# A cross-attention and gated-MLP kernel: the splits of the scores and of the state attention share three buffers, a group's two splits stand together, and the state block's input is split in halves

## The chip, the cores and the metric

The kernel runs on one core of a Trainium2 chip. A core has TensorE (PE in the profile, with PEld for its weight loads), VectorE (DVE), ScalarE (ACT), GpSimd (POOL) and SyncE (SP), which here issues nearly all transfers. The metric is the device time of one execution in microseconds; lower is better.

## The reference

For each of 8 batches and 8 heads there are 512 rows of `x` and 32 rows of `state`, 64 wide. The attention goes both ways: `xread = softmax(scale * x @ state^T) @ state`, and `sread = softmax(scale * state @ x^T) @ x`. Both are joined along the rows, the heads are laid side by side (512 wide, 544 rows per batch, 4352 in all), and two dense stages follow in float32:

```
...
    gate = 1.0 / (1.0 + np.exp(-(x @ w_gate)))
    val = x @ w_val
    return (gate * val @ w_out).astype(np.float32)
...
    h = x @ w_in
    r = np.maximum(h, 0.0)
    g = r * r
    return (g @ w_out).astype(np.float32)
```

The first has 1536 hidden columns, the second 2048.

## The kernel before

Every float32 matmul is made of three: both operands are split into a high part (fp32r, an ACT cast) and the rest (a subtraction), and `mm3` (lines 182 to 184) runs high by high, high by low and low by high.

**The first dense stage** is a list of 108 units. A unit is one slice of 128 hidden columns of one block of rows. Units 0 to 95 are blocks of `x` (512 rows, one batch each; batches 0 to 3 in two halves of six units, then batches 4 to 7 with twelve units each); units 96 to 107 are the state block, the 256 state rows of all batches. `front_x` makes gate and value in PSUM (`psg`, `psv`), a sigmoid on ACT (line 550), a product and its split on DVE and ACT (lines 556, 189, 190); `back1` multiplies by the output weights into four accumulators (`acc`). The units of `x` never form `xread`: the state rows are multiplied by the weights beforehand (`state_weights`, stored by `store_g`, loaded again by `load_g`, split by `split_gw`, lines 536 and 537), and `front_x` takes the attention weights `a` as its other operand.

**The scores** of a batch (`att_a`; stages A2, A3, A4 of `group_stages`, two groups of heads per batch) transpose `x`, split it into `xth` and `xtl` (lines 307 and 308), multiply it with `diag`, the state rows on a diagonal, and make the softmax `a`. They also store the raw scores in memory.

**The state attention** of a batch (`att_b`) has, per group: LN loads rows of `x` (`xn`, line 274), LS loads scores (`e2`, line 350), B4 is the softmax (exp in line 359), B5 transposes the result (`ps_e2`, line 373) and splits it (`et`, lines 376 and 377), SX0 and SX1 split the two halves of `xn` into `xs` (high part on ACT, line 386; low part on POOL, line 387), B60 and B61 multiply `et` by `xs` (line 398) and add up the parts (lines 409 to 411), and B7 transposes the sum (line 420) and copies it into `xs_t` (lines 426 and 428), which is the input of the state block. `xn`, `xs`, `et`, `e2`, `tmp` and the transposed sum have one buffer each; the small PSUM tiles of all these stages share two banks, tag `at`. The splits of the scores have two buffers for each part, `xth` and `xtl`.

**The state block** (`front_s`, `back1`) needs `split_states`, which splits the whole of `xs_t` (four slices of 256 columns) in one cast (line 564) and one subtraction (line 565), and the weights `ws` that `load_gv` fetches (line 570).

**The order.** A queue, sorted by position, gives the places of all side work among the units; one unit is six steps. `att_a` of batch 4 + i is spread over the units from 33 + 7i, `att_b` of batch b over 5.4 units from 45 + 5b, so that its last entry is due at unit 85.2. `ORDER_A` and `ORDER_B` list the stages of a batch, a dash being an empty place; every place takes an equal share of the 5.4 units. The weights of the second dense stage are converted meanwhile (`prep_steps`, units 30.6 to 90). `close_gen` and `open_x_after_att` close memory pools just before the state block and open those of the second stage in their place. A planner then fixes the order of each engine's instructions from the positions and its own cost estimates. A buffer of a tag passes from one tile to the next in program order.

Of the kernel before, what the change touches and what calls it, by code (L numbers as in the profile page):

```python
# [8 lines left out]
F32 = mybir.dt.float32  # L9
F32R = mybir.dt.float32r  # L10
# [8 lines left out]
P = 128  # L19
# [13 lines left out]
def kernel(  # L33
# [12 lines left out]
    nc = tc.nc  # L46
    B, H, S, D = x.shape
    NS = state.shape[2]
    DM = H * D
    DF1 = w_gate.shape[1]  # L50
    DF2 = w_in2.shape[1]
    KD = DM // P
# [4 lines left out]
    NT = S // P  # L57
    NPAIR = H // 2
    NSTATE = B * NS
# [30 lines left out]
    xs_t = xs_p.tile([P, KD, NSTATE], F32, name="xs_t")  # L90
# [90 lines left out]
    def mm3(ps, lh, ll, rh, rl, start, stop, more=False):  # L181
        nc.tensor.matmul(ps, lh, rh, start=start, stop=False, skip_group_check=more)  # L182
        nc.tensor.matmul(ps, lh, rl, start=False, stop=False, skip_group_check=more)  # L183
        nc.tensor.matmul(ps, ll, rh, start=False, stop=stop, skip_group_check=more)  # L184

    def split_g(g32, n):
        gh = gs_p.tile([P, S], F32R, tag="gh", name="gh")
        gl = gs_p.tile([P, S], F32R, tag="gl", name="gl")
        nc.scalar.copy(out=gh[:, :n], in_=g32[:, :n])  # L189
        nc.vector.tensor_sub(out=gl[:, :n], in0=g32[:, :n], in1=gh[:, :n].bitcast(F32))  # L190
        return gh, gl
# [4 lines left out]
    att = ctx.enter_context(ExitStack())  # L196
    once_p = att.enter_context(tc.tile_pool(name="once", bufs=1))
    xq_p = att.enter_context(tc.tile_pool(name="xq", bufs=1))
    xn_p = att.enter_context(tc.tile_pool(name="xn", bufs=1))
    xx_p = att.enter_context(tc.tile_pool(name="xx", bufs=2))  # L200
    f_p = att.enter_context(tc.tile_pool(name="f2k", bufs=2))

    st_t = once_p.tile([P, 2, NPAIR, 2, P], F32R, name="st_t")
# [3 lines left out]
    nc.gpsimd.memset(diag.bitcast(U32), 0)  # L207

    def load_states(m):
        raw = f_p.tile([P, DM], F32, tag="xs", name="sraw", bufs=1)  # L210
        for i in range(BM):
            nc.sync.dma_start(
                out=raw[NS * i : NS * (i + 1)].rearrange("n (h d) -> n h d", h=H),
                in_=state[BM * m + i].rearrange("h n d -> n h d"),
            )
        return raw
# [65 lines left out]
    def group_stages(b, g):  # L282
# [12 lines left out]
        def a2(p):  # L295
            def run():
                if by_pe:
                    xf = at_p.tile([P, S], F32, tag="at", name="ps_xt")
                    for t in range(NT):
                        ts = slice(t * P, (t + 1) * P)  # L300
                        nc.tensor.transpose(xf[:, ts], loaded_x[b, g][:, p, t, :], ident)
                else:
                    xf = f_p.tile([P, S], F32, tag="xf", name="xf", bufs=1)
                    nc.vector.transpose(xf, loaded_x[b, g][:, p, :])
                h = xx_p.tile([P, S], F32R, tag="xth", name="xth")
                l = xx_p.tile([P, S], F32R, tag="xtl", name="xtl")
                nc.scalar.copy(out=h, in_=xf)
                nc.vector.tensor_sub(out=l, in0=xf, in1=h.bitcast(F32))
                v["xt", p] = (h, l)

            return run
# [70 lines left out]
        def sx(p):  # L382
            def run():
                xn = loaded_xn[b, g][:, :, NT * p : NT * (p + 1), :]
                xs = f_p.tile([P, 2, 2, NT, D], F32R, tag="xs", name="xs", bufs=1)
                nc.scalar.copy(out=xs[:, 0], in_=xn)
                nc.gpsimd.tensor_sub(out=xs[:, 1], in0=xn, in1=xs[:, 0].bitcast(F32))
                v["xs", p] = xs

            return run  # L390
# [44 lines left out]
    ORDER_A = "LX.0 - - - A20.0 A21.0 LX.1 A3.0 - A4.0 - A20.1 A21.1 A3.1 - A4.1".split()  # L435

    ORDER_B = (
        "LN.0 LS.0 - - - B4.0 SX0.0 - B5.0 LS.1 - B60.0 SX1.0 LN.1 - B61.0 B4.1 SX0.1 - B5.1 "
        "B7.0 - B60.1 SX1.1 - B61.1 - B7.1"
    ).split()  # L440

    def attention(b):
# [116 lines left out]

    s_parts = {}  # L560

    def split_states():
        t = two["sp"].tile([P, 2, KD, NSTATE], F32R, name="sp")
        nc.scalar.copy(out=t[:, 0], in_=xs_t)
        nc.vector.tensor_sub(out=t[:, 1], in0=xs_t, in1=t[:, 0].bitcast(F32))
        s_parts["a"] = t

    def load_gv(ch, c):
        w = two["S"].tile([P, 2, 512], F32R, tag="w", name="ws")
# [3 lines left out]
    def front_s(b, f):  # L573
        ch, ff = divmod(f, FC)
        n = NSTATE
        t = s_parts["a"]
        out_ps = []
        for i in range(2):
            ps = mm_p.tile([P, S], F32, tag="mm", name="psg" if i == 0 else "psv")
            cols = slice((2 * ff + i) * P, (2 * ff + i + 1) * P)  # L580
            for k in range(KD):
                w = gv[ch, k][:, :, cols]
                mm3(ps[:, :n], w[:, 0], w[:, 1], t[:, 0, k], t[:, 1, k], k == 0, k == KD - 1)
            out_ps.append(ps)
            if i == 0:
                sg = g_p.tile([P, S], F32, tag="sg", name="sg")
                nc.scalar.activation(out=sg[:, :n], in_=ps[:, :n], func=AF.Sigmoid)
            step()
        g32 = g_p.tile([P, S], F32, tag="g32", name="g32")
        nc.vector.tensor_mul(out=g32[:, :n], in0=out_ps[1][:, :n], in1=sg[:, :n])  # L590
        step()
        return split_g(g32, n)
# [41 lines left out]
    two = {}  # L634
# [309 lines left out]
    def spread(fns, start, end):  # L944

        for i, fn in enumerate(fns):
            queue.append((STEPS * (start + (end - start) * i / max(len(fns), 1)), len(queue), fn))
# [3 lines left out]
    def step():  # L951
        count[0] += 1
        while queue and queue[0][0] <= count[0]:
            queue.pop(0)[2]()

    raw = load_states(0)
    att_a, att_b = {}, {}
    for b in range(B):
# [24 lines left out]
    for ch in range(3, NCH):  # L983
        spread(chunk_steps(ch, 0, outs[ch]), 11.5 + 4 * (ch - 3), 15.5 + 4 * (ch - 3))
    second = []
    spread([lambda: second.append(load_states(1))], 21.5, 21.5)
    spread([lambda: prep_states(second.pop())], 23.5, 23.5)
    for ch in range(NCH):
# [7 lines left out]
    u_s = at_unit[B, 0]  # L996
# [3 lines left out]
        open_x()  # L1000

    spread([close_gen], u_s - 0.6, u_s)
    spread([split_states], u_s - 0.55, u_s)
    spread([open_x_after_att], u_s - 0.5, u_s)
    spread([close_gen2], 30.5, 30.5)
    prep = prep_steps()
# [27 lines left out]
    for i, (b, f, lo, hi) in enumerate(units):  # L1034
        count[0] = STEPS * i
        g = (front_x if b < B else front_s)(b, f)
        drain(0)
        held.append(lambda b=b, f=f, lo=lo, hi=hi, g=g: back1(b, f, lo, hi, g))
# [71 lines left out]
```

## Time and profile before

| | us |
|---|---|
| median of 3 runs | 1499.65 (1497.92 to 1499.72) |
| profiled execution, its own time | 1500.54 |
| its span, first to last instruction | 1498.8 |
| TensorE busy in the span | 1431.0 |
| mean granted TensorE clock | 0.985 of full speed |

The profile is one execution. A row of a timeline gives start, duration, engine, line, operation, output and inputs, and the idle time of the engine before it with what ended it. PE rows of one kind that follow each other are merged. A row of a stretch gives for each engine its busy time in it.

### The profile page before, as it was taken

How to read it: one execution, taken by the hardware profiler on the slowest of the kernel's cores; microseconds unless marked ns; L12 is line 12 of the kernel's file. 1: busy time of each engine (PE TensorE's matmuls, PEld its weight loads, DVE VectorE, ACT ScalarE, POOL GpSimd, SP SyncE). 2: the span in 40 equal slices, each digit the busy share in tenths (PEclk: the TensorE clock that was granted, in tenths of full speed). 3: DMA queues.
4: the chain of work that ended last, by engine and by line, in shares of the span. 5: the costliest groups of instructions: out<-in, count | busy, mean ns of one | idle time of the engine just before them, and what ended most of it. 6: DMA issues, size and time to landing. Idle time of an engine off the chain costs nothing.

```text
span 1498.8 us, 19379 instructions
## 1 busy us (share of the span) xinstructions
PE 1431.0 (95%) x6552; PEld 1176.9 (79%) x6552; DVE 940.2 (63%) x1579; ACT 748.8 (50%) x1291; POOL 246.0 (16%) x216
## 2 busy tenths in 40 slices
PE   5879999999999989999899999999999999999998
PEld 3558878887787677888798788888888888888887
DVE  7986887578889987555536655734575356433443
ACT  6865876456678887666424522332242223232211
POOL 1112213232344544333101100000000000000000
PEclk9889999999999999999999999999999999999999
DMA  9984799699999864333677844644365443645442
GB/s 265 341 263 120 229 328 339 210 363 292 323 296 286 254 211 145 95 113 92 242 271 250 274 158 147 217 146 143 133 227 188 151 152 134 222 124 195 155 145 80
DMA packets 244595, 311.68 MB, mean 208 GB/s; under 512 B 105361, under 2 KB 152977, under 8 KB 244497
## 3 DMA queue, kind: packets, MB, share of 16 engines
q1 hardware_dynamic: 242224, 309.66, 63.8%
q10 hardware_dynamic: 2272, 0.79, 0.3%
q8 instruction: 52, 0.85, 0.2%
q14 instruction: 47, 0.38, 0.1%
HBM read 221.25 MB, written 89.13 MB: 207 GB/s over the span
## 4 chain that ended last, share of the span: by engine, by line
PE 72%; DVE 10%; ACT 7%; DMA 7%; issue 3%; SPq 1%; POOL 0%; ACTq 0%; DVEq 0%; POOLq 0%
PE o L182 8%; PE o L183 8%; PE o L184 8%; PE px L183 4%; PE px L182 4%; PE px L184 4%; PE acc L183 4%; PE acc L184 3%; PE acc L182 3%; DMA raw<-in_moe_w_out_dram 2%; PE psg L182 2%; PE psg L183 2%; PE psg L184 2%; PE psv L182 2%; PE psv L183 2%
## 5 line engine op out<-in xcount | busy, mean ns | idle before, releaser
L182 PE MATMUL o<-wo,g2h 128*128 128x512 f32 x512 | 198.6, 390 | 3.7 <-DMA wo<-wo 3.0
L183 PE MATMUL o<-wo,g2h 128*128 128x512 f32 x512 | 199.1, 389 | 0.0
L184 PE MATMUL o<-wo,g2l 128*128 128x512 f32 x512 | 193.9, 389 | 0.0
L537 POOL TENSOR_TENSOR gg<-gi,gg 128x512 fp32r<-128x512 f32 x96 | 135.3, 1412 | 350.5 <-ACT gg L536 284.2
L183 PE MATMUL acc<-gl,o 128*128 128x512 f32 (+1 forms) x432 | 164.4, 381 | 3.7 <-DVE gl L190 3.7
L184 PE MATMUL acc<-gh,o 128*128 128x512 f32 (+1 forms) x432 | 163.0, 378 | 0.0
L841 ACT CAST g2h<-c 128x512 fp32r<-128x512 f32 x96 | 59.3, 622 | 178.8 <-DVE c L837 178.8
L182 PE MATMUL acc<-gh,o 128*128 128x512 f32 (+1 forms) x432 | 139.3, 380 | 0.6 <-DVE y L624 0.4
L893 DVE TENSOR_TENSOR y<-o,y 128x512 f32<-128x512 f32 x102 | 68.5, 688 | 103.5 <-PE o L184 102.8
L182 PEld LDWEIGHTS o<-wo,g2h 128*128 128x128 f32 x512 | 96.1, 188 | 24.9 <-ACT p L826 3.0
L184 PEld LDWEIGHTS o<-wo,g2l 128*128 128x128 f32 x512 | 96.1, 188 | 19.8
L183 PEld LDWEIGHTS o<-wo,g2h 128*128 128x128 f32 x512 | 96.2, 188 | 19.5
L190 DVE TENSOR_TENSOR gl<-g,gh 128x512 fp32r<-128x512 f32 (+1 forms) x108 | 88.4, 818 | 36.3 <-ACT gh L189 35.8
L182 PE MATMUL px<-xh,wi 128*128 128x512 f32 x256 | 99.8, 390 | 0.0
L183 PE MATMUL px<-xl,wi 128*128 128x512 f32 x256 | 99.7, 389 | 0.0
L184 PE MATMUL px<-xh,wi 128*128 128x512 f32 x256 | 99.6, 389 | 0.0
L183 PEld LDWEIGHTS acc<-gl,o 128*128 128x128 f32 x432 | 81.3, 188 | 21.3 <-DVE gl L190 6.9
L182 PEld LDWEIGHTS acc<-gh,o 128*128 128x128 f32 x432 | 80.6, 189 | 17.4 <-DVE y L624 1.1
L184 PEld LDWEIGHTS acc<-gh,o 128*128 128x128 f32 x432 | 81.3, 188 | 14.6
L182 PE MATMUL psg<-a,gg 128*128 128x512 f32 x192 | 78.6, 409 | 14.8 <-ACT sg L550 12.1
L556 DVE TENSOR_TENSOR g<-psv,sg 128x512 f32<-128x512 f32 x96 | 65.6, 683 | 35.4 <-PE psv L184 21.6
L189 ACT CAST gh<-g 128x512 fp32r<-128x512 f32 (+1 forms) x108 | 64.3, 596 | 40.4 <-DVE g L556 23.0
(188 smaller groups left out, 3268.7 us busy)
## 6 DMA issues: line engine op xcount, KB each, us to landing
wi<-wi SPq DMA_DIRECT2D x256, 256.0 KB, 3.1
wo<-wo SPq DMA_DIRECT2D x64, 512.0 KB, 5.5
gd<-go SPq DMA_DIRECT2D x192, 128.0 KB, 4.4
gi<-gd SPq DMA_DIRECT2D x96, 256.0 KB, 4.0
wi<-wa SPq DMA_DIRECT2D x32, 512.0 KB, 5.0
wd<-w SPq DMA_DIRECT2D x24, 512.0 KB, 5.1
ws<-wd SPq DMA_DIRECT2D x24, 512.0 KB, 6.7
raw<-in_moe_w_out_dram SPq DMA_DIRECT2D x20, 512.0 KB, 6.2
```

What stands on the lines that cost most here:

```text
L182: nc.tensor.matmul(ps, lh, rh, start=start, stop=False, skip_group_check=more)
L183: nc.tensor.matmul(ps, lh, rl, start=False, stop=False, skip_group_check=more)
L184: nc.tensor.matmul(ps, ll, rh, start=False, stop=stop, skip_group_check=more)
L189: nc.scalar.copy(out=gh[:, :n], in_=g32[:, :n])
L190: nc.vector.tensor_sub(out=gl[:, :n], in0=g32[:, :n], in1=gh[:, :n].bitcast(F32))
L537: nc.gpsimd.tensor_sub(out=t[:, 1], in0=src, in1=t[:, 0].bitcast(F32))
L556: nc.vector.tensor_mul(out=g32, in0=ps, in1=sg)
L841: nc.scalar.copy(out=h, in_=c)
L893: nc.vector.tensor_add(out=y, in0=acc, in1=y)
```

## The change

The splits of the scores (`xth`, `xtl`) become one tile of twice the size, and the splits of the state attention (`xs`) take tiles of the same tag: three shared buffers, where there were two pairs for the scores and one `xs`. The memory is the same. In `ORDER_B` the two splits of a group stand together ahead of B5, B60 and B61 follow each other, and the next group's load of `xn` stands earlier; the list has 26 places in place of 28. The state rows loaded for `prep_states` now take the buffer of `e2`. `split_states` runs once for each half of `xs_t` (slices 0 and 1, which group 0 of each batch fills, and slices 2 and 3), and `front_s` reads the halves.

```diff
-    xx_p = att.enter_context(tc.tile_pool(name="xx", bufs=2))
+    xx_p = att.enter_context(tc.tile_pool(name="xx", bufs=3))
...
-        raw = f_p.tile([P, DM], F32, tag="xs", name="sraw", bufs=1)
+        raw = f_p.tile([P, DM], F32, tag="e2", name="sraw", bufs=1)
...
-                h = xx_p.tile([P, S], F32R, tag="xth", name="xth")
-                l = xx_p.tile([P, S], F32R, tag="xtl", name="xtl")
+                t = xx_p.tile([P, 2, S], F32R, tag="xx", name="xt")
+                h, l = t[:, 0, :], t[:, 1, :]
...
-                xs = f_p.tile([P, 2, 2, NT, D], F32R, tag="xs", name="xs", bufs=1)
+                xs = xx_p.tile([P, 2, 2, NT, D], F32R, tag="xx", name="xs")
...
-        "LN.0 LS.0 - - - B4.0 SX0.0 - B5.0 LS.1 - B60.0 SX1.0 LN.1 - B61.0 B4.1 SX0.1 - B5.1 "
-        "B7.0 - B60.1 SX1.1 - B61.1 - B7.1"
+        "LN.0 LS.0 - - B4.0 SX0.0 SX1.0 - B5.0 LN.1 LS.1 - B60.0 B61.0 - B4.1 SX0.1 SX1.1 - B5.1 "
+        "B7.0 - B60.1 B61.1 - B7.1"
...
-    def split_states():
-        t = two["sp"].tile([P, 2, KD, NSTATE], F32R, name="sp")
-        nc.scalar.copy(out=t[:, 0], in_=xs_t)
-        nc.vector.tensor_sub(out=t[:, 1], in0=xs_t, in1=t[:, 0].bitcast(F32))
-        s_parts["a"] = t
+    def split_states(g):
+        t = two["sp"].tile([P, 2, 2, NSTATE], F32R, name=f"sp{g}")
+        src = xs_t[:, 2 * g : 2 * g + 2, :]
+        nc.scalar.copy(out=t[:, 0], in_=src)
+        nc.vector.tensor_sub(out=t[:, 1], in0=src, in1=t[:, 0].bitcast(F32))
+        s_parts[g] = t
...
-                mm3(ps[:, :n], w[:, 0], w[:, 1], t[:, 0, k], t[:, 1, k], k == 0, k == KD - 1)
+                mm3(ps[:, :n], w[:, 0], w[:, 1], s_parts[k // 2][:, 0, k % 2], s_parts[k // 2][:, 1, k % 2], k == 0, k == KD - 1)
...
-    spread([split_states], u_s - 0.55, u_s)
+    for g in range(2):
+        spread([lambda g=g: split_states(g)], u_s - 0.55, u_s)
```

## Rows read from the trace of the kernel before

**Rows 1.** The page: busy shares, and PE in 40 equal slices

```profile
PE 1431.0 (95%) x6552; PEld 1176.9 (79%) x6552; DVE 940.2 (63%) x1579; ACT 748.8 (50%) x1291; POOL 246.0 (16%) x216
...
PE   5879999999999989999899999999999999999998
```

**Rows 2.** Stretches: us; busy PE, PEld, DVE, ACT, POOL; clock; DMA share, GB/s

```profile
460.00:500.00 40.00, 36.42 (x155) 27.84 (x154) 39.07 (x66) 35.22 (x58) 22.42 (x21) 0.96 0.92 272
500.00:540.00 40.00, 34.35 (x146) 26.30 (x146) 32.77 (x60) 32.32 (x56) 18.45 (x15) 0.98 0.87 260
540.00:580.00 40.00, 36.24 (x159) 27.99 (x159) 35.59 (x63) 31.54 (x54) 16.33 (x13) 0.98 0.47 159
...
660.00:700.00 40.00, 40.00 (x192) 33.51 (x191) 23.49 (x46) 27.89 (x50) 15.76 (x12) 1.00 0.38 108
```

**Rows 3.** The timeline where the units of x end and the state block begins

```profile
724.29 3.84 SPq L570 DMA_DIRECT2D ws<-wd  x8
...
730.16 0.64 PE L398 MATMUL ps_sr<-xs,et 128*128 128x256 f32 x4
...
732.25 0.30 PE L420 MATMUL ps_so<-ident,sw 128*128 128x128 f32 x1 [1.45 <-DVE sw L411]
...
734.05 0.18 ACT L426 COPY xs_t<-ps_so 64x32 f32<-64x32 f32 x1
...
734.78 1.04 ACT L564 CAST sp<-xs_t 128x1024 fp32r<-128x1024 f32 x1
...
735.87 0.48 PE L182 MATMUL psg<-sp,ws 128*128 128x256 f32 x1 [3.32 <-ACT sp L564]
...
737.30 0.58 PE L183 MATMUL psg<-sp,ws 128*128 128x256 f32 x1 [0.73 <-DVE sp L565]
...
743.63 0.39 PE L184 MATMUL pz<-xh,wi 128*128 128x512 f32 x1
...
743.86 0.28 PE L182 MATMUL psg<-sp,ws 128*128 128x256 f32 x1
...
744.81 0.28 PE L184 MATMUL psg<-sp,ws 128*128 128x256 f32 x1
```

**Rows 4.** Two of the stretches of 2 us there, columns as in Rows 2

```profile
736.00:738.00 2.00, 1.27 (x5) 0.97 (x6) 2.00 (x4) 0.86 (x2) 0.00 (x0) 0.50 0.96 362
...
744.00:746.00 2.00, 2.00 (x19) 2.00 (x18) 0.00 (x0) 0.38 (x1) 0.00 (x0) 1.00 1.06 384
```

**Rows 5.** The timeline of one group of the state attention, batch 5

```profile
646.07 0.64 PE L398 MATMUL ps_sr<-xs,et 128*128 128x256 f32 x4
...
649.05 0.62 ACT L386 CAST xs<-xn 128x512 fp32r<-128x512 f32 x1
...
649.75 1.29 POOL L387 TENSOR_TENSOR xs<-xn,xs 128x512 fp32r<-128x512 f32 x1 [0.49 <-ACT xs L386]
...
650.16 1.02 DVE L411 TENSOR_TENSOR sw<-tmp 64x128 f32<-64x128 f32 x1
...
653.82 0.64 PE L398 MATMUL ps_sr<-xs,et 128*128 128x256 f32 x4
```

**Rows 6.** By line, up to 668 us: the sigmoids, one for each unit

```profile
L550 ACT ACTIVATE sg<-psg x86: 563/599/656, 56.2 to 664.9; 128x512 f32<-128x512 f32 x86
```

**Rows 7.** By tile and line: duration min/median/max ns, first and last start

```profile
L420 PE MATMUL ps_so<-ident,sw x16: 270/271/328, 433.2 to 732.2; 128*128 128x128 f32 x16
...
L386 ACT CAST xs<-xn x32: 605/618/624, 240.1 to 727.9; 128x512 fp32r<-128x512 f32 x32
...
L222 PE MATMUL ps_st<-ident,sraw x8: 270/346/446, 6.8 to 236.3; 128*128 128x128 f32 x8
...
L274 SPq DMA_DIRECT2D xn<-in_x_dram x32: 372/574/1262, 6.7 to 718.7; - x32
...
L359 ACT ACTIVATE e<-e,nm x16: 697/724/726, 44.3 to 715.1; 128x512 f32<-128x512 f32 x16
```

**Rows 8.** What PE waited for, whole span: total us, times, longest

```profile
PE psg L182 <- ACT sg L550: 12.1, 13, 3.0
...
PE ps_xt L301 <- DVE xtl L308: 3.9, 1, 3.9
```

More of the change, by code (lines that the diff above doesn't have):

```diff
@@ L575, in front_s @@
         n = NSTATE
-        t = s_parts["a"]
         out_ps = []
```

## The prediction, made before the changed kernel ran

> **What bounds the kernel now.** I read the page first. TensorE is busy 95% of the span, and its slices show where it is not: in the first three, and nowhere else for long [rows 1]. From slice 4 on, time can only be won where TensorE waits. The stretches name two such places. Between 460 and 580 us it is busy 36.42, 34.35 and 36.24 us of 40, so it loses 3.58 + 5.65 + 3.76 = 13.0 us in 120; DVE is busy 107.4 us of those 120 and ACT 99.1. From 660 to 700 it is busy 40.00 of 40 [rows 2]. The second place is the seam between the units of x and the state block, which I read in the timeline [rows 3]. The last unit of x is done, and TensorE runs the last state-attention product, from 730.16 to 730.80. The state block cannot follow: its input needs the sum of that product, a transpose at 732.25, copies that end at 734.23, and a cast of all four slices from 734.78. The first state matmul is at 735.87, the next needs the subtraction and starts at 737.30. After these waits the engine works at half its rate: the granted clock is 0.50, the 1.2 GHz level, at 736 to 738, and 1.00 again, 2.4 GHz, at 744 to 746 [rows 4].
>
> So the chain that sets the seam is the state attention, which is late. The last of its entries is due at unit 85.2. The sigmoids count the units: the 86th, that of unit 85, starts at 664.9 [rows 6]; the last transpose is at 732.2 (line 420) [rows 7]. The chain ends some 67 us, 11 units of about 6 us, behind its place, and behind the last unit of x.
>
> **Why it is late, and what the change removes.** One group shows it [rows 5]. The product of the first half starts at 646.07. It frees `xs`, ACT fills it again at 649.05, POOL subtracts from 649.75 to 651.04, and the second product starts at 653.82: 7.75 us between two products that have 0.64 us of work each. There are 16 such groups. A second buffer lets both splits be ready before the first product. What is left between the two is their own work, below 1 us, so a group saves about 7 us, the 16 groups about 110 us: an estimate from this one group. The chain needs 11 units, 67 us, to be on time, and only the distance from 732 to about 724, some 8 us, for the seam. Even a third of the saving clears it.
>
> **The seam, step by step** [rows 3]. From 730.80 to 743.86 TensorE does 24 state matmuls, six matmuls of the next stage (`pz`) and one transpose. At full pace a state matmul takes 0.119 us (eight steps in the 0.95 us from 743.86 to 744.81) and a 512-column one 0.23 us (743.63 to 743.86). That is 24 x 0.119 + 6 x 0.23 + about 0.1 = 4.3 us. It took 13.06. The loss is 8.7 us, waits and half pace together.
>
> What comes late next is the weights `ws`. Their eight loads are issued from 724.29 over 3.84 us, and nothing in the change moves them. The rows bound the landing only from above: the first weights were there by 735.87. If they land in time the price is 0; if as late as the first state matmul of before, it is 5.1 us and only 3.6 us of the gain stay. Transfers run at 362 GB/s here [rows 4]; two chunks of 0.5 MB ahead of the first product take about 3 us, and four, a unit's set, about 6. So the first are there when TensorE comes at 730.8, and the fourth comes about when it is needed. I take 1 us.
>
> The halves of `split_states` are two casts and two subtractions of half the size, in the place of one of 1.04 us; done under the last unit's matmuls they cost TensorE nothing. Without that cover, the first product would wait for half a cast, and its input would still be whole: that is a gain of half a us on the seam as it is, not a loss.
>
> **The other edits.** The state rows move to the buffer of `e2`. Buffers pass in program order: `xs` had its first tile cast at 240.1, right behind the last transpose of the second set of state rows at 236.3, although its data were loaded at 6.7 [rows 7]. Now `e2` will stand behind these rows: the first exp, at 44.3, moves past 236. It is 0.72 us of ACT and, among sigmoids, two table loads, some 3.3 us where TensorE is busy without gaps; I take 0, and up to 3 us if its ACT time falls on a sigmoid.
>
> The load of `xn` stands earlier. In SP's queue it waits until both splits have read the old rows, and the unit loads (`gi`) stand behind it. The two splits now follow each other, so that wait ends sooner than before: 0.
>
> The scores get three buffers where they had two pairs, and share them. At start-up the one long wait for a score split is for the PSUM bank of a transpose (`ps_xt` behind `xtl`, 3.9 us) [rows 8], which the change leaves; I take 0, with 2 us either way for the order. Around units 56 to 60 two score splits and two state splits want three buffers; a late score split holds up one product, and the scores are due at unit 84 at the latest for the last batch: 0.
>
> POOL now gets two subtractions of 1.29 us in a row. The row at 650.16 shows the price of one: a DVE addition that reads two tiles of SBUF lasts 1.02 us and ends with POOL's subtraction [rows 5]. The Trainium skill, page "SBUF — State Buffer", section "Who interferes with whom", says that such a DVE instruction and a GpSimd one that reads SBUF exclude each other, and that the later one blocks in full; by that rule two in a row could hold a DVE instruction for 2.6 us, and 32 holds of another 1.3 us would be 42 us of DVE time. The trace agrees with the lock, not with that sum. The number of subtractions is the same, and the addition that was hit came right behind the split in the old order; in the new one it does not. I take 0.
>
> **The unknown cost** is the stretch from 460 to 580. A chain that is on time puts up to two batches of state attention, now run after 580, into it. Per group ACT has two casts of `xs` (0.62), an exp (0.72) and its two table loads, and small copies: with four such groups some 28 us of ACT, where 120 - 99.1 = 21 us are free [rows 2]. Either the conversion of the second stage's weights gives way, which is due only by unit 90, and nothing is lost; or sigmoids come later, for which PE waited 12.1 us in all [rows 8]. From below: work that is on time no longer stands ahead of the units on ACT, and half of the 13.0 us, 6.5, could go. From above: stalls double, +13. I take 0, since the conversion can give way.
>
> **The sum.** 1500.54 (the profiled execution, 1.7 us over its span) - 8.7 + 1.0 = 1492.8. The median shown is 0.9 us below that execution; by it 1491.9, say **1492**.
>
> **The rivals.** "No difference" is within 0.2%, 3.0 us, which is about what a measurement of this kernel can tell.
> *The chain stays late* (12%): only 2.0 us of the 7.75 are the split itself, and 2.8 us pass between POOL's end and the second product [rows 5]. If TensorE's place for it in the planner's order, or the two `at` banks shared with the scores, set the pace, the group ends after unit 95 again. It decides when the last transpose is still after 730. Time: 1499.7. TensorE full from 660 to 700 speaks for it: no repeated gap asks for a buffer there. The page "Perfetto Trace Analysis" of the Trainium skill, section "Optimization Strategy", takes a gap that repeats on the engine that should be full as the sign of missing buffers; here the gap comes once, at the end of the chain, so by that sign nothing would be won.
> *Crowding takes it back or more* (22%): the stalls of 460 to 580 grow. At 5 to 10 us more the result is within 3 us of before (8%); from 10.7 us more on it is slower, doubled stalls give 1492 + 13 = 1505 (14%). For it: DVE at 39.07 of 40 in one stretch. Against: all of that work must be done before 730 anyway, and the weights can wait.
> *Crowding eases* (10%): half the stalls go, 1492 - 6.5 = 1485.5.
>
> **How the numbers follow.** The forecast has 56%, with a range of its own of 1489 to 1496 (1491 to 1496 with a price of the loads from 0 to 5.1 us, and 2 us of start-up on the early side). Faster by over 0.2%: 0.56 + 0.10 = 0.66; within it 0.12 + 0.08 = 0.20; slower 0.14. The range is 1485 to 1501: it takes in the eased case and the late chain, and leaves out most of the slower case and the tail of the eased one.
>
> **What would show it.** Right: the last `ps_so` at about unit 86 to 90, long before the last unit of x; second products within 1 us of the first; state matmuls straight behind the last `acc`, clock 1.00 through the seam; a wait on `ws` of a us at most. Wrong: a last `ps_so` still at the seam; stalls on sigmoids above 13 us at 460 to 580; the state block waiting for `ws` as long as it did for `sp`.

## The result, and the profile after

The changed kernel takes 1517.53 us, the median of 4 runs (1515.08 to 1520.18), against 1499.49 us in the same comparison: the measured ratio is 1.0123, with a 95% interval of 1.0108 to 1.0139. That is 18 us slower, where 7.7 us faster was forecast. The profiled execution took 1520.18 us, its span 1518.4.

Two rows of the page, busy shares and PE in 40 slices, answer to [rows 1]:

```profile
PE 1436.5 (95%) x6552; PEld 1176.8 (78%) x6552; DVE 943.3 (62%) x1580; ACT 747.5 (49%) x1292; POOL 245.5 (16%) x216
...
PE   5869999999997989899999999999999999999998
```

The busy times are nearly the same. The slices show a new hole, the 13th, at 456 to 493 us. The stretches of the changed kernel, columns as in [rows 2], show two places:

```profile
460.00:500.00 40.00, 31.44 (x126) 23.63 (x125) 35.06 (x68) 29.59 (x53) 19.46 (x19) 0.87 0.91 270
500.00:540.00 40.00, 37.55 (x162) 28.76 (x162) 37.92 (x65) 32.61 (x58) 20.57 (x16) 1.00 0.83 234
...
620.00:660.00 40.00, 36.89 (x172) 28.83 (x171) 23.67 (x48) 27.32 (x51) 16.18 (x12) 1.00 0.36 94
660.00:700.00 40.00, 35.75 (x169) 28.71 (x168) 23.55 (x48) 27.90 (x50) 14.92 (x12) 0.98 0.35 104
```

From 460 to 500 PE is busy 31.44 us where it was 36.42, at a clock of 0.87 where it was 0.96. From 620 to 700 it loses 3.11 + 4.25 us where it lost nothing: [rows 2] has 660 to 700 of the kernel before, and its stretch ahead of that is

```profile
620.00:660.00 40.00, 40.00 (x194) 33.47 (x194) 22.44 (x44) 27.27 (x48) 14.28 (x11) 1.00 0.33 93
```

The sigmoids (line 550) count the units, so their start, kernel against kernel, says where time goes. The sigmoid of unit 55 is 0.3 us later than before, that of unit 58 15.8, of unit 65 10.5, of unit 75 14.0, of unit 80 22.8 and of unit 95 24.7 us. The whole span is 19.6 us longer, so what stands behind the start of that last sigmoid gave back 24.7 - 19.6 = 5.1 us. Not all of it is the seam. The last state matmul starts at 791.2 us before and at 812.8 in the change, in rows by tile and line of either kernel:

```profile
L184 PE MATMUL psv<-sp,ws x48: 281/283/415, 740.0 to 791.2; 128*128 128x256 f32 x48
```

```profile
L184 PE MATMUL psv<-sp,ws x48: 277/283/415, 752.4 to 812.8; 128*128 128x256 f32 x48
```

That is 68.9 us behind the sigmoid of unit 95 before, and 65.8 in the change: 3.1 us less. But eight matmuls of the state attention, five transposes and two matmuls of the unit, which TensorE did in this stretch before, are done ahead of it in the change; at full pace they are some 1.8 us, an estimate from the pace of such rows. The other 2.0 us of the 5.1 lie behind the last state matmul, where the profiles of all kernels of this document lie anywhere from 705 to 714 us. There are three things to explain: a loss of some 11 us at units 55 to 60, another of some 10 at units 75 to 85, and a seam that gave 1 to 1.5 us in place of 7.7.

By tile and line, as in [rows 7], the changed kernel shows what the chain of the state attention does:

```profile
L420 PE MATMUL ps_so<-ident,sw x16: 270/272/415, 435.3 to 713.4; 128*128 128x128 f32 x16
...
L222 PE MATMUL ps_st<-ident,sraw x8: 272/347/447, 6.7 to 237.2; 128*128 128x128 f32 x8
...
L359 ACT ACTIVATE e<-e,nm x16: 722/723/728, 250.1 to 692.9; 128x512 f32<-128x512 f32 x16
```

The last transpose starts at 713.4, just ahead of the sigmoid of unit 89 (714.01). Before it was behind unit 95 [rows 7].

**The seam.** The timeline where the state block begins answers to [rows 3]:

```profile
747.04 0.60 ACT L550 ACTIVATE sg<-psg 128x512 f32<-128x512 f32 x1 [2.72 <-PE psg L184]
747.53 1.13 ACT L565 CAST sp<-xs_t 128x512 fp32r<-128x512 f32 x2
748.38 3.73 SPq L571 DMA_DIRECT2D ws<-wd  x8
749.02 1.28 DVE L566 TENSOR_TENSOR sp<-xs_t,sp 128x512 fp32r<-128x512 f32 x2
...
751.76 0.31 PE L182 MATMUL psg<-sp,ws 128*128 128x256 f32 x1
...
755.25 0.38 PE L182 MATMUL psg<-sp,ws 128*128 128x256 f32 x1 [0.75 <-DMA ws<-wd]
...
757.80 0.39 PE L182 MATMUL psg<-sp,ws 128*128 128x256 f32 x1 [1.57 <-DMA ws<-wd]
...
760.37 0.58 PE L182 MATMUL psg<-sp,ws 128*128 128x256 f32 x1 [1.60 <-DMA ws<-wd]
```

The input is split under the last unit, and the state matmuls no longer wait for it. They wait for `ws`. The trace has the landing of each of the eight loads issued from 748.38: 751.64, 753.19, 755.21, 756.48, 757.76, 759.05, 760.33 and 761.58 us. PE's three waits end at 755.25, 757.80 and 760.37, just behind the third, the fifth and the seventh. So the loads land one after the other, from the third on some 1.27 us apart, which for 512 KB is about 412 GB/s; but the four chunks that the first state unit needs are the first, third, fifth and seventh of them. `load_gv` queues the chunks of the first two weight sets at the same places, so that the two sets alternate, and the fourth chunk of the first set is there 12 us after the first issue. Stretches there, as in [rows 4]: the transfers run at 418 GB/s, PE is idle most of the time, and when the last chunk is there the clock is at 0.50, the 1.2 GHz level.

```profile
758.00:760.00 2.00, 0.77 (x6) 0.56 (x5) 0.00 (x0) 0.00 (x0) 0.00 (x0) 0.97 1.02 418
760.00:762.00 2.00, 1.63 (x7) 1.44 (x7) 0.00 (x0) 0.38 (x1) 0.00 (x0) 0.50 0.81 205
...
764.00:766.00 2.00, 2.00 (x11) 2.00 (x11) 0.00 (x0) 0.38 (x1) 0.00 (x0) 0.50 1.09 332
```

The timeline has the state matmuls at full pace again from this row on:

```profile
766.75 0.28 PE L183 MATMUL psv<-sp,ws 128*128 128x256 f32 x1
```

From 751.76 to 766.75 TensorE runs 46 state matmuls and eight of `acc` with 512 columns. At the full pace of [rows 3], 0.119 and 0.23 us each, that is 7.3 us. It took 15.0. So 7.7 us are lost here, where the same working gave 8.7 before: one wait stands in the place of another.

**Units 75 to 85.** The timeline of one group in the changed kernel, beside [rows 5]:

```profile
618.80 0.64 PE L398 MATMUL ps_sr<-xs,et 128*128 128x256 f32 x4
...
619.74 0.63 PE L398 MATMUL ps_sr<-xs,et 128*128 128x256 f32 x4
...
622.35 1.47 POOL L537 TENSOR_TENSOR gg<-gi,gg 128x512 fp32r<-128x512 f32 x1 [5.32 <-ACT gg L536]
622.70 0.36 ACT L409 COPY tmp<-ps_sr 64x256 f32<-64x256 f32 x1
622.83 1.54 DVE L190 TENSOR_TENSOR gl<-g,gh 128x512 fp32r<-128x512 f32 x1 [0.16 <-ACT gh L189]
...
623.77 1.74 POOL L387 TENSOR_TENSOR xs<-xn,xs 128x512 fp32r<-128x512 f32 x1
624.29 0.41 DVE L410 TENSOR_TENSOR tmp<-ps_sr,tmp 64x256 f32<-64x256 f32 x1
624.73 0.93 DVE L411 TENSOR_TENSOR sw<-tmp 64x128 f32<-64x128 f32 x1
...
625.75 0.37 ACT L409 COPY tmp<-ps_sr 64x256 f32<-64x256 f32 x1 [2.16 <-DVE sw L411]
626.14 1.28 ACT L550 ACT_TABLE_LOAD   x1
...
627.43 0.60 ACT L550 ACTIVATE sg<-psg 128x512 f32<-128x512 f32 x1
```

The two products are 0.94 us apart where they were 7.75. Both results then want the one `tmp`. ACT copies the first at 622.70; the second copy has to wait until DVE has made both additions of the first, and ends that wait of 2.16 us at 625.75. ACT works in order: the sigmoid of the unit and its table load stand behind that copy, and PE waits for the sigmoid. Over 560 to 730 us the waits of ACT show it as their largest row, which the kernel before does not have, and over 580 to 720 us the waits of PE for the sigmoids are theirs (total, times, longest; before, 0.3 us, once):

```profile
ACT tmp L409 <- DVE sw L411: 16.6, 10, 2.2
```

```profile
PE psg L182 <- ACT sg L550: 8.9, 9, 2.3
```

### The profile page after: what moved, and what is told of

It is laid out like the page before. It is cut to its first block, busy times and chain, and to the rows that moved or that the text cites. A ratio compares the mean times of both kernels' runs of the same rounds, so it can differ in the third digit from the quotient of the medians.

```text
span 1518.4 us, 19425 instructions
## 1 busy us (share of the span) xinstructions
PE 1436.5 (95%) x6552; PEld 1176.8 (78%) x6552; DVE 943.3 (62%) x1580; ACT 747.5 (49%) x1292; POOL 245.5 (16%) x216
## 4 chain that ended last, share of the span: by engine, by line
PE 65%; DMA 10%; DVE 10%; ACT 8%; issue 3%; SPq 2%; POOL 1%; ACTq 0%; DVEq 0%; POOLq 0%
PE o L182 8%; PE o L183 8%; PE o L184 8%; PE px L183 4%; PE px L182 4%; PE px L184 4%; PE acc L183 3%; PE acc L184 3%; PE acc L182 3%; PE psg L182 2%; PE pz L183 2%; PE pz L182 2%; PE pz L184 2%; PE psg L184 2%; PE psg L183 2%
## 5 line engine op out<-in xcount | busy, mean ns | idle before, releaser
L182 PEld LDWEIGHTS o<-wo,g2h 128*128 128x128 f32 x512 | 96.2, 188 | 22.8 <-ACT g2h L841 1.0
L184 PEld LDWEIGHTS o<-wo,g2l 128*128 128x128 f32 x512 | 96.0, 188 | 19.8
L183 PEld LDWEIGHTS o<-wo,g2h 128*128 128x128 f32 x512 | 96.2, 188 | 19.5
L183 PEld LDWEIGHTS acc<-gl,o 128*128 128x128 f32 x432 | 81.3, 188 | 26.5 <-DVE gl L190 11.8
L182 PEld LDWEIGHTS acc<-gh,o 128*128 128x128 f32 x432 | 81.3, 189 | 19.6 <-ACT gh L189 3.2
```

## The experiments

Two theories stood at the start. **T**: the two products of a group that follow each other make ACT hold (the second copy into the single `tmp` waits for DVE, a sigmoid is queued behind it). **C**: the chain is served too early and too densely, whatever its order. They are told apart by lateness unit by unit (us, start of the sigmoid against that of before) and by PE's idle time. Lateness and idle time are from the profiled executions, one of each kernel; the last column is the measured ratio to the kernel before in the same comparison, with its 95% interval, which is not exactly the ratio of the two medians. "Before" of the four comparisons was 1498.06, 1499.89, 1499.58 and 1500.18 us.

| run | unit 55 | 58 | 65 | 75 | 80 | 95 | PE idle 420-580 | 580-720 | ratio |
|---|---|---|---|---|---|---|---|---|---|
| before | 0 | 0 | 0 | 0 | 0 | 0 | 13.0 | 0.8 | 1 |
| the change | +0.3 | +15.8 | +10.5 | +14.0 | +22.8 | +24.7 | 18.9 | 9.9 | 1.0123 [1.0108, 1.0139] |
| e1_old_order | +1.2 | +1.7 | -0.1 | +4.0 | +11.0 | +12.9 | 14.3 | 6.6 | 1.0040 [1.0013, 1.0067] |
| e2_tmp_dve | +0.5 | +12.0 | +11.9 | +12.3 | +11.0 | +11.1 | 19.2 | 1.1 | 1.0032 [1.0011, 1.0054] |
| e7_spread | -4.6 | +5.6 | +7.2 | +10.5 | +18.7 | +19.5 | 22.5 | 9.4 | 1.0166 [1.0133, 1.0199] |
| e8_apart | +2.6 | +6.6 | +1.7 | +8.9 | +9.3 | +10.7 | 15.4 | 4.2 | 1.0071 [1.0051, 1.0091] |
| e3_halves | -0.6 | +0.5 | +0.6 | +0.5 | +0.5 | +0.5 | 14.5 | 0.7 | 1.0002 [0.9989, 1.0014] |
| e5_new_list | -1.4 | +12.2 | +12.0 | +11.6 | +11.0 | +11.8 | 19.7 | 0.0 | 1.0077 [1.0059, 1.0096] |
| e11_before_tmp_dve | -2.8 | -4.4 | -0.5 | +3.0 | +3.4 | +3.1 | 14.7 | 2.1 | 1.0044 [1.0027, 1.0061] |
| e12_old_list_tmp_dve | -0.8 | -0.2 | -2.6 | +2.4 | +3.4 | +4.2 | 12.8 | 2.7 | 1.0041 [1.0026, 1.0056] |
| e13_places | -0.8 | -0.4 | -0.4 | -0.4 | -0.4 | -0.5 | 13.1 | 0.8 | 1.0001 [0.9991, 1.0011] |
| e14_rows_early | +0.4 | +0.7 | -0.1 | -0.3 | -0.5 | -0.7 | 13.7 | 1.1 | 0.9995 [0.9986, 1.0004] |
| e15_half_unit | +6.2 | +3.0 | +0.3 | +3.0 | +3.1 | +3.6 | 13.7 | 1.0 | 1.0010 [1.0000, 1.0021] |
| e16_pairs | -1.3 | +12.3 | +12.1 | +13.9 | +13.1 | +13.9 | 19.8 | 2.5 | 1.0082 [1.0066, 1.0099] |
| e17_apart_tmp_dve | -2.5 | +1.2 | +0.8 | +4.6 | +3.8 | +4.0 | 16.7 | 2.0 | 1.0013 [1.0000, 1.0026] |
| e18_products | +4.0 | +10.7 | +8.8 | +8.3 | +6.3 | +7.0 | 16.9 | 1.3 | 1.0010 [0.9996, 1.0024] |
| e19_splits | -0.6 | -4.1 | -0.3 | +2.5 | +2.3 | +1.8 | 15.5 | 0.2 | 0.9996 [0.9985, 1.0007] |

**The changed kernel with one thing taken back.** e1_old_order: the shared buffers and the halves, with the list of before.

```diff
-        "LN.0 LS.0 - - B4.0 SX0.0 SX1.0 - B5.0 LN.1 LS.1 - B60.0 B61.0 - B4.1 SX0.1 SX1.1 - B5.1 "
-        "B7.0 - B60.1 B61.1 - B7.1"
+        "LN.0 LS.0 - - - B4.0 SX0.0 - B5.0 LS.1 - B60.0 SX1.0 LN.1 - B61.0 B4.1 SX0.1 - B5.1 "
+        "B7.0 - B60.1 SX1.1 - B61.1 - B7.1"
```

> The changed kernel with the old list of the state attention: three shared buffers, state rows in the buffer of e2, halves, but SX1 again behind B60, and B60 and B61 apart. Theory T (the two products together make ACT hold: the second copy into the one tmp buffer waits for DVE's additions, with a sigmoid queued behind it): the waits of ACT on sw (16.6 us from 580 to 716 in the changed kernel) are gone and the loss of units 75 to 87 (13 us) with them: 1500 to 1506. Theory C (the chain is served too early, whatever its list): still above 1511, since the buffers alone make it early. If the buffers do no harm at all and the list all: 1493 to 1500.

1506.55 us. The first loss is gone by unit 65 (-0.1), the second is there: ACT waits for `sw` 13.6 us, 8 times, and units 75 to 80 lose. Theory T had expected these waits to go with the list. The shared buffers alone bring the products together in the planner's order, whatever the list says: from 600 to 680 us, six groups' products start 0 to 0.94 us apart.

e2_tmp_dve: in the changed kernel the second product's copy is made by DVE, so ACT has nothing to wait for.

```diff
-                nc.scalar.copy(out=tmp, in_=sv[64:128])
+                (nc.vector.tensor_copy if p else nc.scalar.copy)(out=tmp, in_=sv[64:128])
```

> The changed kernel, but the copy of the second product's part into tmp is done by DVE, so that ACT no longer waits for tmp. Theory T: the waits of ACT on sw fall from 16.6 us to about 0 and the time to 1506 to 1511. Theory C: the waits fall too, but the time stays within 1514 to 1520, since the units are held up by the amount of state-attention work and not by this wait.

1503.02 us, below the range of either theory. The wait of ACT for `sw` is gone, and the second loss with it. Its stretches, columns as in [rows 2]:

```profile
620.00:660.00 40.00, 40.00 (x194) 33.22 (x193) 25.51 (x53) 28.28 (x49) 17.68 (x13) 1.00 0.43 113
660.00:700.00 40.00, 39.78 (x197) 33.16 (x196) 27.33 (x55) 29.61 (x52) 15.49 (x12) 1.00 0.40 113
```

PE is full again where the change had lost 7.4 us. The first loss stays: +12.0 at unit 58, +11.1 at unit 95. So theory T holds for the second loss and says nothing of the first.

e7_spread (the batches of the state attention six units apart) and e8_apart (the splits together, the products three places apart):

```diff
-        start = 45 + 5 * b
+        start = 45 + 6 * b
```

```diff
-        "LN.0 LS.0 - - B4.0 SX0.0 SX1.0 - B5.0 LN.1 LS.1 - B60.0 B61.0 - B4.1 SX0.1 SX1.1 - B5.1 "
-        "B7.0 - B60.1 B61.1 - B7.1"
+        "LN.0 LS.0 - - - B4.0 SX0.0 SX1.0 - B5.0 LN.1 LS.1 - B60.0 - - B61.0 B4.1 SX0.1 SX1.1 - B5.1 "
+        "B7.0 - B60.1 - - B61.1 - B7.1"
```

> The changed kernel with the state attention of batch b from unit 45 + 6b in place of 45 + 5b: the same list, less of it in each unit, the last entry due at 92.4. Theory C: fewer stalls from 460 to 580 and after, 1502 to 1510, with the last transpose near unit 94. Theory T: every group still has its wait on tmp, 1513 to 1519.

> The changed kernel with a list of 28 places in which the two splits of a group stand together, but B60 and B61 are three places apart, as before. Theory T: the second copy finds tmp free, waits of ACT on sw below 4 us, 1503 to 1509. Theory C: 1513 to 1519, as early and as dense as the changed kernel.

e7 takes 1523.81 us, above the range of either theory. Later service (the last `ps_so` at 725.0) is no help: idle time at 420 to 580 is 22.5 us, and ACT still waits 12.6 us for `sw`. Theory C finds no support. e8 takes 1509.57: the first loss shrinks to 1.7 us at unit 65, the wait for `sw` to 9.2 us only, where theory T had expected less than 4, since behind 570 us the planner sets its products together all the same.

**The kernel before with one thing added.** e3_halves has only the split of the state block's input in halves; e5_new_list only the new list, with one split buffer; e11_before_tmp_dve only DVE's copy, as a control to e2. e12_old_list_tmp_dve is e1 with that copy.

```diff
-    spread([split_states], u_s - 0.55, u_s)
+    for g in range(2):
+        spread([lambda g=g: split_states(g)], u_s - 0.55, u_s)
```

> The kernel before, with the state block's input split in halves and nothing else changed. At the seam the first cast takes 0.62 us in place of 1.04, and the first products need only the first half, which is complete earlier: about 1 us of the 8.7 us lost there, 1497 to 1499. If the halves add to the loss of the changed kernel: above 1502.

> The kernel before with the new list alone: one xs buffer, so that the second split still waits for the first product. Theory T (products that follow each other make ACT hold): the products cannot follow each other, so no waits of ACT on sw and 1495 to 1502. If the places of the new list are the harm by themselves: above 1508.

> Control: the kernel before with the copy of the second product's part done by DVE. Before, ACT does not wait for tmp, so nothing to win: 1496 to 1501. If it gains more than 4 us, the gain of the same edit on the changed kernel (14 us) was not that of the wait on tmp alone.

> The changed kernel with the old list and with the second copy by DVE. With the old list ACT still waited 13.6 us for sw, since both splits are ready and the planner lets the products follow each other. Theory T: these waits go, 1494 to 1500, below the changed list with the same edit (1503). If sharing the buffers costs by itself, in the stretch from 420 to 580: 1501 to 1506.

The halves are worth nothing (1499.22). The new list costs 10.7 us (1510.57) without a second buffer and without a wait for `sw`: it is the first loss by itself, +12.2 at unit 58, and no more behind it. The control, of which nothing was expected, costs 5.2 us (1505.09), 3 of them before unit 95. So DVE's copy is not free there; if it costs something in the changed kernel too, which no run tells apart, the single `tmp` costs more than e2 against the change shows. e12 (1506.45) has little of either loss in its units, +4.2 at unit 95, and still is 6.6 us slower; a single wait for a `wo` load in the second stage takes 4.9 us there (3.0 us in two waits before), the rest was not followed up.

**Which part of the list.** All on the kernel before, with its one split buffer. e13_places takes out two empty places, e14_rows_early moves only the load of rows, e15_half_unit shifts every batch by half a unit, e16_pairs makes both pairs on the old 28 places.

```diff
# e13_places
+        "LN.0 LS.0 - - B4.0 SX0.0 - B5.0 LS.1 - B60.0 SX1.0 LN.1 - B61.0 B4.1 SX0.1 - B5.1 "
+        "B7.0 - B60.1 SX1.1 B61.1 - B7.1"
# e14_rows_early
+        "LN.0 LS.0 - - - B4.0 SX0.0 - B5.0 LN.1 LS.1 - B60.0 SX1.0 - B61.0 B4.1 SX0.1 - B5.1 "
+        "B7.0 - B60.1 SX1.1 - B61.1 - B7.1"
# e15_half_unit
+        start = 45.5 + 5 * b
# e16_pairs
+        "LN.0 LS.0 - - - B4.0 SX0.0 SX1.0 - B5.0 LS.1 - B60.0 B61.0 LN.1 - B4.1 SX0.1 SX1.1 - B5.1 "
+        "B7.0 - B60.1 B61.1 - - B7.1"
```

> The kernel before with two empty places taken out of its list (26 places in place of 28), the order of the stages as it was. Left to tell: which part of the new list costs the 11 us or so around units 55 to 60. If it is the denser spacing of a batch's stages, the sigmoid of unit 60 comes 10 us or more later than before and the time is 1508 to 1512. If it is the order of the stages (the two products together), unit 60 is within 3 us of before and the time within 3 us of 1499.9. If any shift of the side work moves the plan there, something between, 1502 to 1508.

> The kernel before with only the next group's load of rows moved from behind the second split to ahead of the load of scores, as the new list has it. Only a transfer changes its place, so every theory that puts the cost on ACT, DVE and PE expects no change: 1499 to 1501, unit 60 within 2 us. If the load in SP's queue is what costs (it waits there for the old rows to be read, and the unit loads stand behind it), PE waits for gi or gd and the time is above 1505.

> The kernel before with every batch of the state attention put half a unit later (45.5 + 5b for 45 + 5b), the list untouched. A neutral shift: if the cost at units 55 to 60 belongs to the new list itself, this is within 3 us of 1499.9. If any shift of the side work against the units costs there, as the plan of before only happens to fit, it is 1505 or more, with the loss at units 55 to 60 again and no single wait behind it.

> The kernel before with the stages in pairs as in the new list (both splits, then both products) on the old 28 places, one split buffer, the loads where they were. If the pairs cost, the sigmoid of unit 60 is 10 us or more later than before and the time 1508 to 1512; if the denser spacing does, unit 60 is within 3 us and the time within 3 us of 1499.9. With one split buffer the second split still waits for the first product, so no wait of ACT on the additions behind the first product (sw) is expected.

1499.95, 1498.92, 1500.95 and 1512.21 us. Spacing, load and a shift move the median by -0.7 to +1.4 us; the pairs cost 12.6, and they do so at units 57 and 58. Then each half of the pairs alone, and the changed kernel without either loss:

```diff
# e18_products
+        "LN.0 LS.0 - - - B4.0 SX0.0 - B5.0 LS.1 - B60.0 SX1.0 B61.0 LN.1 - B4.1 SX0.1 - B5.1 "
+        "B7.0 - B60.1 SX1.1 B61.1 - - B7.1"
# e19_splits
+        "LN.0 LS.0 - - - B4.0 SX0.0 SX1.0 - B5.0 LS.1 - B60.0 LN.1 - B61.0 B4.1 SX0.1 SX1.1 - B5.1 "
+        "B7.0 - B60.1 - B61.1 - B7.1"
# e17_apart_tmp_dve: the list of e8_apart with the copy of e2_tmp_dve
```

> The kernel before with only the products of a group together in the list (first product, second split, second product in following places), the splits as they were. If the products are the costly half of the pairs, the sigmoid of unit 60 is 10 us or more late and the time 1508 to 1513; if the splits are, unit 60 is within 4 us and the time 1498 to 1503.

> The kernel before with only the splits of a group together in the list (the second ahead of the softmax transposes), the products at their old distance. With one buffer the second split still waits for the first product, so ACT can hold it, and what stands behind it, until then. If the splits are the costly half, unit 60 is 10 us or more late and the time 1508 to 1513; if the products are, unit 60 is within 4 us and the time 1498 to 1503.

> The changed kernel with both costs found so far taken away: the splits of a group together but its products three places apart (28 places), and the second product's copy into tmp made by DVE, so that no sigmoid stands behind it on ACT. If the two costs are the whole loss, the sigmoid of unit 95 is within 4 us of before, the seam keeps its gain of about 4 to 5 us, and the time is 1495 to 1501, the first version not slower than before. If the shared buffers cost something of their own, or DVE's copy does (6.6 us in the kernel before with that copy alone), it is 1503 to 1507 again.

The splits alone cost nothing (1499.53). The products alone make the hole at unit 58 (+10.7), as expected of the costly half; but 3.7 us of it are back by unit 95, that profiled execution was itself 4.3 us above the median, and the median is 1501.38, 1.2 us over before and not the 1508 or more that was expected. Its twelve executions lie between 1497.65 and 1506.70 us. By the medians neither half alone costs what the pairs cost together (12.6 us). Two stretches show the two halves, e18_products and then e19_splits:

```profile
480.00:500.00 20.00, 17.62 (x65) 14.02 (x65) 16.60 (x28) 15.13 (x27) 11.46 (x13) 0.78 0.89 263
```

```profile
480.00:500.00 20.00, 17.44 (x80) 13.85 (x81) 17.22 (x32) 17.13 (x27) 9.97 (x12) 1.00 0.86 240
```

PE is busy nearly alike, 17.6 and 17.4 us, but runs 65 rows of matmuls in the one and 80 in the other: the clock is 0.78 against 1.00.

e17 has neither loss (unit 65 at +0.8, unit 80 at +3.8) and takes 1501.47 us, at most 0.3% over before by the interval. (The 6.6 us that its expectation gives for DVE's copy in the kernel before are those of e12; e11 measured 5.2.) Its stretches, its last transpose by tile, and the largest of PE's waits at the seam:

```profile
620.00:660.00 40.00, 40.00 (x196) 33.55 (x195) 26.05 (x52) 28.60 (x50) 16.31 (x13) 1.00 0.37 101
660.00:700.00 40.00, 40.00 (x197) 33.40 (x196) 27.85 (x54) 25.60 (x46) 13.83 (x11) 1.00 0.39 112
```

```profile
L420 PE MATMUL ps_so<-ident,sw x16: 270/271/328, 429.7 to 702.9; 128*128 128x128 f32 x16
```

```profile
PE psg L182 <- DMA ws<-wd: 3.4, 3, 1.6
```

The chain is over at 702.9. Unit 95 is 4.0 us late, the span 1498.1 against 1498.8, so 4.7 us come back behind it, and they pay for the 4.0 and no more. The seam's share is small again: from 731.08 to 745.48 us the same 46 and eight matmuls take 14.4 us for 7.3 us of work, a loss of 7.1 against 8.7 before. Some 1.8 us are the work that is now done ahead of unit 95's sigmoid, as in the change. No version here beats the kernel before.

## Why the prediction was wrong, point by point

**Right: the chain was late, and the second buffer mends that.** The last `ps_so` was forecast at unit 86 to 90 and came at 89. The products of ten of the 16 groups start within 1 us of each other, and from 590 us on all of them within 1.2 us; five groups ahead of that are still 2.7 to 10.3 us apart. The state matmuls follow the last `acc` straight away. But the seam was not worth what the forecast took from it, with either of the two losses (the change) or without them (e17).

**Mis-sized: the price of `ws`.** It was put at 1 us within 0 to 5.1. By the forecast's own working the seam of the change loses 7.7 us (7.1 in e17), so the price is 7.7 and the gain of the seam 1.0 us in place of 7.7. It was assumed that the four chunks that a unit needs come one behind the other, in about 6 us. The rate was as high as assumed, but the loads of two weight sets alternate, and the fourth chunk came after 12 us. PE waits 0.75 + 1.57 + 1.60 = 3.9 us, about as long as it did for `sp` (3.32 + 0.73), which was named as a sign of being wrong; the rest is the matmuls at a clock of 0.50 behind the waits, which the price did not hold. The trace of before could have told: there the seventh load lands at 736.86, 12.6 us after the first is issued. Loading the first set ahead of the second was not tried.

**Failed: the unknown cost of 460 to 580, taken as 0.** It was 10.5 us by unit 65; the list alone costs 10.7 us (e5), its pairs alone 12.6 (e16). Of the work that the on-time chain brings, the forecast said that the conversion of weights could give way. Instead PE, ACT and DVE each work in a fixed order, and the steps of the chain stand in it. This is the changed kernel at the first loss, in its timeline:

```profile
472.91 0.66 PE L373 MATMUL ps_e<-ident,e 128*128 128x128 f32 x4 [1.17 <-ACT go L466]
...
475.92 0.62 ACT L684 CAST wu<-c 128x512 fp32r<-128x512 f32 x1 [1.56 <-DVE c L131]
...
476.56 1.28 ACT L550 ACT_TABLE_LOAD   x1
...
477.85 0.60 ACT L550 ACTIVATE sg<-psg 128x512 f32<-128x512 f32 x1
...
478.34 0.58 ACT L376 CAST et<-ps_e 128x512 fp32r<-128x512 f32 x1
...
478.95 0.69 DVE L377 TENSOR_TENSOR et<-ps_e,et 128x512 fp32r<-128x512 f32 x1 [0.34 <-ACT et L376]
...
479.70 1.86 PE L398 MATMUL ps_sr<-xs,et 128*128 128x256 f32 x8 [2.02 <-DVE et L377]
```

The softmax is transposed by 473.6, but ACT is held by a cast of the weights that waits for DVE (line 684), then by a sigmoid, and `et` is ready at 479.6. Both products stand next in PE's order and wait 2.02 us for it. The conversion did not give way; it stood ahead. Two-us stretches of the changed kernel show what follows such a wait:

```profile
478.00:480.00 2.00, 0.30 (x2) 0.30 (x3) 1.66 (x4) 2.00 (x5) 0.00 (x0) 1.00 0.82 225
480.00:482.00 2.00, 1.83 (x9) 1.54 (x8) 2.00 (x5) 2.00 (x5) 0.00 (x0) 0.50 1.03 373
...
490.00:492.00 2.00, 0.00 (x0) 0.00 (x0) 0.70 (x3) 1.51 (x4) 2.00 (x3) 0.56 1.36 172
492.00:494.00 2.00, 1.68 (x6) 1.57 (x7) 0.58 (x1) 1.98 (x5) 1.81 (x5) 0.50 0.77 260
```

PE is busy 0.30 us of 2 and then runs at the 1.2 GHz level; the same again at 490 to 494. So the loss is the idle time (40 - 31.44 = 8.56 us from 460 to 500 against 3.58 before) and the slow matmuls behind it. No single wait carries it: from 420 to 580 PE waits 5.3 us for `g`, 2.7 for `e`, 2.3 for `et` and 2.1 for sigmoids, where before the largest was 6.4 for sigmoids. In e16_pairs, with one buffer, the waits in the same place are others. Its timeline:

```profile
477.50 2.08 PE L182 MATMUL acc<-gh,o 128*128 128x512 f32 x4 [3.27 <-ACT gh L189]
...
486.15 0.74 PE L398 MATMUL ps_sr<-xs,et 128*128 128x256 f32 x4 [2.06 <-POOL xs L387]
```

The loss is the same 12 us. What the kernels with it have in common is the group whose products stand in this stretch. In e17_apart_tmp_dve, without the loss, its two products are these, in the timeline of PE:

```profile
470.34 0.64 PE L398 MATMUL ps_sr<-xs,et 128*128 128x256 f32 x4
...
478.68 0.85 PE L398 MATMUL ps_sr<-xs,et 128*128 128x256 f32 x4
```

They are 8.3 us apart. Before it is 12.8 us (473.1 and 485.9), in e8 7.0, in e1, e3, e11 to e15 and e19 9.8 to 13.9: unit 58 is 6.6 us late at most in all of these. In the change and e2 the two start together, in e5, e16 and e18 within 2.7 to 3.2 us, and unit 58 is 10.7 to 15.8 us late. The close products start late, too, the first at 479.7 to 485.0 where the others have it at 470.3 to 477.4; in e7, whose phase differs, they are 5.7 us apart from 482.6, and 10 us go between units 55 and 58. One more thing goes with the loss: the group ahead of this one has its products 9.8 to 15.2 us apart in these six kernels, and 6.6 to 8.4 us in all others, so that the lateness may begin there. So it is shown that products set together in this stretch go with the loss, that the pairs of the list bring them there with either buffers, and that spacing, the load and a shift do not. Open is whether the close products are the cause or a mark of it, what in the planner's order moves the first product back, and why the loss of e18 is mostly gone by the end, while that of e16 stays.

**Failed: the list was priced at nothing.** The two splits in a row were looked at, and the load of `xn`; that B60 and B61 follow each other was not. It puts two results into one `tmp`, and the wait that the second `xs` removed moved there, 16.6 us of it on the engine that also makes the sigmoids. e1 shows that the shared buffers do this without the new list, e2 that it is the copy on ACT. By e2 it costs 14.5 us between the medians, which are of two comparisons. A second `tmp`, the direct remedy, was not tried.

**Right in sum, wrong in place: POOL and DVE.** DVE's busy time rises by 3.1 us in all, far from 42. But the rows at 622.83 (1.54 us, where this subtraction has a median of 0.68) and 624.73 (0.93, where the next one takes 0.28) overlap POOL's subtractions at 622.35 and 623.77, and both stand between the two copies into `tmp`. The Trainium skill, page "SBUF — State Buffer", section "Who interferes with whom", says that a DVE instruction with two inputs in SBUF contends with a GpSimd one that reads SBUF, for a lock that only one of them holds. The trace agrees in that both are longer beside a subtraction of POOL; the price here is paid by the wait of ACT.

**Right: the small edits.** The first exp moved from 44.3 to 250.1 behind the state rows, and unit 40 is 0.8 us late, unit 50 2.6 us early; halves are worth nothing (e3).

**The rivals.** The time lies on the side of the crowding rival, with a sign of its list (idle time in 460 to 580 up, 18.9 us against 13.0), but beyond its 1505: doubled stalls were its bound, and neither the clock behind them, nor the second loss, nor the real price of `ws` was in it. The rule that the late-chain rival named (the Trainium skill, page "Perfetto Trace Analysis", section "Optimization Strategy": a gap that repeats can mean that there is no room for the next tile, by the count of buffers or the size of tiles) fits the changed kernel rather than the one before: the gaps of 620 to 700 go when ACT no longer waits for the single `tmp` (e2). That a second `tmp` would close them was not tried.

## What to carry to other kernels

When a buffer is doubled, look for the next single buffer behind it, and for what is queued on the engine that will now wait there; a copy of 0.37 us held a sigmoid and with it TensorE. Work that is late but fits in the gaps may be better left late: here 1 to 2 us at the seam stood against 4 to 25 us in the units. Before a wait is taken away, look at what ends next, and in which order its transfers are issued: here the weights came almost as late as the input had. And an order that is planned with every engine nearly full is to be priced by the waits it makes in each queue, not by the sum of the busy times.

## What the runs showed that was not expected

Eight loads of 512 KB, issued within 3.7 us, landed one after the other, the first 3.3 us after its issue and from the third on some 1.27 us apart, at about 412 GB/s: the four that were wanted first stood at every second place of the queue, and so came 2.6 us apart. PE's idle time costs more than itself: with equal busy time in 480 to 500 (17.6 and 17.4 us) e18 ran 65 rows of matmuls at a clock of 0.78 and e19 80 at 1.00. And edits without a share in the two losses moved the median too (e14 -0.7, e15 +1.4, e11 +5.2 us), so a gain of a few us in the order of this kernel can be lost to the edit that brings it.
